# Attention with a relative bias, then a maxout FFN: the left-over keys' band by DMA, one pair loaded straight, one pair's bands and the first FFN block moved

## The chip, the cores and the metric

One core of one Trainium2 chip. The metric is the device time of one execution in microseconds; the kernel before has three timed runs.

## The reference

Eight batches of eight heads, 576 positions, 64 columns per head. Scores get a bias that depends on the distance of query and key alone (32 buckets, all distances from 128 on in one), then softmax, then the values. The result, 4608 tokens of 512, goes through a maxout FFN.

```python
scores = scale * np.matmul(q, k.transpose(0, 1, 3, 2))
...
bias = bias_table[bucket]
scores = scores + bias.transpose(2, 0, 1)[None, :, :, :]
attn = np.exp(scores - np.max(scores, axis=-1, keepdims=True))
attn = attn / (np.sum(attn, axis=-1, keepdims=True) + 1e-09)
x = np.matmul(attn, v)   # then (tokens, heads * columns)
h = np.maximum(np.maximum(x @ w1, x @ w2), x @ w3)
out = h @ w_out
```

## The kernel before, in words

**Attention.** Heads go in pairs, `hp` 0 to 3; the text calls them pair 0 to pair 3. Queries and keys lie transposed in `qT` and `kT`. For each pair PE (TensorE) makes scores with the keys on the partitions (`sc`), ACT (ScalarE) takes their exponential into `e4` (`e` in the profile), and DVE (VectorE) multiplies in the bias as exp(bias) (`times_band`, `times_band_pair`). Only a band around the diagonal needs that, since far distances share one bucket, whose bias has been taken off. The band's factors are in `hank`, one window of 384 columns for each partition and head, loaded by SP (SyncE) from a small DRAM tensor `w_dr` with a step of one element from partition to partition, and read backwards. Then PE sums the values (`attend`, tile `a`; a column of ones gives the divisor), and DVE divides (`quotients`, a reciprocal and a product into `x_sb`).

**The left-over 64 positions.** 576 is 4 x 128 + 64. The left-over keys of both heads of a pair share one tile: `left_keys` makes their scores (`sct`), ACT writes `el`, and `times_bandt` (L905) multiplies its last 192 columns with `bandt`, whose upper 64 partitions hold the even head and lower 64 the odd one. `make_bandt` (L352) fills `bandt` by two copies on POOL (GpSimd) from `hank`, backwards, so that `times_bandt` reads it forwards. `left_queries` and `times_band_left` do the left-over queries (`scq`).

**FFN.** Blocks of tokens go through three gates (`w_bf`, tiles `ps`): the first product of a block (f) is copied by ACT, the second (m) and third (g) are combined with it by DVE. `add_ffn` puts the products of a block of tokens into `pending`, and `fill(n)` emits them on PE up to a budget of n, between attention's steps. For the first 256 tokens the list is f0; f1 and m0; m1; f2 and m2, and the g's come with the next tokens. f's tile, and that of the transposes `xp` and `tp` of the first batch, come from the same two PSUM banks `ff`.

**Order.** The order on PE, DVE, and for most DMAs is that of the program text. Batch 0 has two passes over its pairs: the first makes the scores of the first 256 queries, the second (the loop behind `products`, L1128) the scores of the other queries, pair by pair, and in between the sums for the first 256. `more_transposes(hp + 1)` there turns the next pair's queries on PE into an `ff` bank, and DVE copies them out (L126, `qT<-tp`). `x_transposes` turns divided results into `xT` for the FFN, with a copy by ACT (L123, `xT<-xp`). In the second pass `bands(2)` stands behind the first quotients of pair 0's step, `bands(3)` behind its second ones, and `add_ffn(0, QS)` with `fill(8)` in pair 3's step.

**Batch 1.** (Batch two in the change's title.) Its queries and keys are not turned by DMA as those of later batches but by PE: `second_transposes(made, hp)` puts a pair into an `sc` bank, DVE copies out the queries and ACT the keys (`kT<-tp`). `load_second` (L1072) loads them on POOL's queue with wider rows (`load_packed`: per partition and head 256 neighbouring elements) into a borrowed part of `xT`, first pair 0, then the rest, and `spread_packed` copies each pair to its place: pair 0 on POOL, the others on DVE. Between them it loads the left-over rows, the second gate's weights and, behind all, values and the third gate's weights.

**Queues.** POOL issues the loads of attention and weights, SP the large band, later the DMA transposes and stores. Each load has one of eight semaphores of its queue kind in turn, and waits for the load that had it before. `go_behind` makes a load wait for an instruction.

Of the kernel before, what the change touches and what calls it, by code (L numbers as in the profile page):

```python
# [12 lines left out]
ALU = mybir.AluOpType  # L13
# [26 lines left out]
def kernel(  # L40
# [12 lines left out]
    nc = tc.nc  # L53
    B, H, S, D = q.shape
    d_model, d_ff = moe_w1.shape
    NB = bias_table.shape[0]
    P = 128
    assert d_model == H * D and S == 576 and D == 64 and NB == 32 and H == 8
    inv_sqrt_d = 1.0 / float(np.sqrt(D))
    HP = H // 2  # L60
    QS = 2 * P
    QM = 2 * QS
    KT = 4
# [8 lines left out]
    BAND = 3 * P  # L72
    HALF = 2 * P - 1
    WL = 2 * HALF + 1
# [17 lines left out]
    inorder = tc.keep_in_program_order  # L92
# [82 lines left out]
    def load_q_tail(b):  # L175
        dst = qtail[b % 2][0 : S - KT * P].rearrange("p g (h d) -> p (g h) d", h=2)
        return in_turn(b, nc.gpsimd.dma_start(out=dst, in_=q[b, :, KT * P : S, :].rearrange("h p d -> p h d")), 64 * H)
# [7 lines left out]
    def load_tail(src, b, h0, h1, dst):  # L185
        return [
            in_turn(
                b, nc.gpsimd.dma_start(out=dst(b, par, h0, h1), in_=tail_part(src, b, h0, h1, par)), 32 * (h1 - h0)
            )
            for par in range(2)  # L190
        ]
# [21 lines left out]
    def go_behind(loads, behind):  # L213

        for load in loads if behind else ():
            tc.add_manual_dep(
                load.ins, behind.ins.name,
                mybir.DependencyInfo(mybir.DependencyClass.Sync, mybir.DependencyReason.DATA),
                reason="these loads go behind the transposes in line",
            )  # L220
# [15 lines left out]
    def load_32(src, h, dst, eng, nt=KT):  # L236
# [4 lines left out]
    k_1, q_1 = (  # L241
        xT[:, c, NTOK - KT * H * D :].rearrange("p (h t d) -> p h t d", t=KT, h=H) for c in (3, 2)
    )

    def load_packed(src, h0, h1, dst):
        part = src[1, h0:h1, 0 : KT * P, :].rearrange("h (p t) d -> p h (t d)", t=KT)
        inorder(nc.gpsimd.dma_start(out=dst[:, h0:h1].rearrange("p h t d -> p h (t d)"), in_=part))

    def spread_packed(hp, eng):
        h = slice(2 * hp, 2 * hp + 2)  # L250
        for dst, src in zip(batch[1], (q_1, k_1)):
            inorder(eng.tensor_copy(dst[:, :, h, :], src[:, h].rearrange("p h t d -> p t h d")))
# [5 lines left out]
    batch = [None] * B  # L258
# [77 lines left out]
    w_dr = dram.tile([H, WL], BF16, name="w_dr")  # L336
# [12 lines left out]

    bandt = const.tile([P, HP, 192], BF16, name="bandt")  # L350

    def make_bandt():  # L352
        for par in range(2):
            r = slice(64 * par, 64 * par + 64)
            c = BAND // 2 - 64 * par
            inorder(nc.gpsimd.tensor_copy(bandt[r, :, :], hank[r, par::2, c : c + 192][:, :, ::-1]))

# [334 lines left out]
    def add_ffn(t0, nt, last=False):  # L694
        portions, left = ffn(t0, nt, last)
        portions[0] = rest + portions[0]
        rest[:] = left
        pending.extend((sum(n for n, _ in p), [fn for _, fn in p]) for p in portions)
# [206 lines left out]

    def times_bandt(hp, el):
        return inorder(nc.vector.tensor_tensor(
            out=el[:, S - 192 : S], in0=el[:, S - 192 : S], in1=bandt[:, hp, :], op=ALU.mult
        ))

    def left_queries(hp, qT, kT, el):
# [12 lines left out]
    divided = {}  # L924
# [100 lines left out]
    def x_transposes(hp, half):  # L1025

        xp = ps_f.tile([P, 2 * CH], BF16, tag="ff", name="xp")
        lo, hi = (0, QS) if half == 0 else (QS, S)
        for q in range(lo // P, -(-hi // P))[::-1]:
            c = min(P * q, S - P) - lo  # L1030
            tr(xp[:, c : c + P], x_sb[0][:, q, P * hp : P * hp + P], ident[:])
        act_copy(xT[:, hp, lo:hi], xp[:, 0 : hi - lo])
# [8 lines left out]
    def next_late():  # L1041
        return late.pop(0)() if late else (lambda: None)
# [20 lines left out]
    def load_w(i):  # L1063
        src = (moe_w1, moe_w2, moe_w3)[i].rearrange("(c p) f -> p c f", p=P)
        for f0, f1 in ((0, QS), (QS, d_ff)) if i else ((0, d_ff),):
            in_turn(0, nc.gpsimd.dma_start(out=w_bf[i][:, :, f0:f1], in_=src[:, :, f0:f1]))
# [3 lines left out]
    wo_bf = const.tile([P, FCH, d_model], BF16, name="wo_bf")  # L1070

    def load_second():  # L1072
        for h0, h1 in ((0, 2), (2, H)):
            load_packed(k, h0, h1, k_1)
            load_packed(q, h0, h1, q_1)
            if h0 == 0:
                load_q_tail(1)
                load_tail(k, 1, 0, H, k_diag)
                load_w(1)
                make_bandt()  # L1080
        spread_packed(0, nc.gpsimd)
        load_v(1, 0, H)
        load_w(2)

# [3 lines left out]
    def bands(hp):  # L1088
        times_band_pair(hp, first_e[hp], 0, 0)
        times_band(hp, first_e[hp], 2, 0, QS, inorder)  # L1090
# [9 lines left out]
    for hp in range(HP):  # L1100
        qT, kT = (x[:, hp, :] for x in qk[0])
        e4, el = e_tiles()
# [29 lines left out]
    for hp in range(HP):  # L1132
        qT, kT = (x[:, hp, :] for x in qk[0])
        if begun:
            e4, el = begun.pop()
            more_transposes(hp + 1)
            scores(qT, kT, e4, 1, 2)
        else:
            e4, el = e_tiles()
            visit(qT, kT, e4, [(1, 0), (1, 2)], (lambda: more_transposes(hp + 1)) if hp + 1 < HP else None)  # L1140

        def keys():
            left_keys(hp, qT, kT, el, QS, S)

        def queries():
            left_queries(hp, qT, kT, el)

        def late_bands(hp=hp, e4=e4):
            times_band(hp, e4, 1, QS, QM, inorder)
            times_band_pair(hp, e4, 2, QS)  # L1150

        if hp == 0:
            keys()
        if hp == 1:
            x_transposes(0, 0)
        quotients = next_late()
        if hp < 2:
            quotients()
            if hp == 0:
                bands(2)  # L1160
            else:
                behind.pop()()
                keys()
            queries()
            if hp == 1:
                x_transposes(1, 0)
            else:
                begun.append(e_tiles())
                scores(*(x[:, 1, :] for x in qk[0]), begun[0][0], 1, 0)
            quotients = next_late()  # L1170
            quotients()
            if hp == 0:
                bands(3)
            behind.append(lambda late_bands=late_bands, hp=hp, el=el: (late_bands(), products(hp, el)))
        else:
            if behind:
                behind.pop()()
            if hp == 3:
                quotients()
                add_ffn(0, QS)  # L1180
                fill(8)
            keys()
            if hp == 2:
                quotients()
            queries()
            late_bands()
            if hp == 2:
                x_transposes(2, 0)
                x_transposes(3, 0)
            else:  # L1190
                begin_qk(2)
                x_transposes(0, 1)
                fill(8, lambda: second_transposes(qk[1], 0))
            products(hp, el)
        late.append(lambda hp=hp, e4=e4, el=el: attend(0, hp, e4, el, 1))
# [235 lines left out]
```

## Time and profile before

| | us |
|---|---|
| median of three runs | 308.22 |
| lowest, highest | 306.51, 308.97 |
| the profiled execution | 307.46 |
| its span, first to last instruction | 305.7 |
| PE busy | 294.5 |
| DVE busy | 206.9 |
| ACT busy | 201.3 |
| POOL busy | 143.7 |

In the profile PE is TensorE's matmuls, DVE VectorE, ACT ScalarE, POOL GpSimd, SP SyncE; L and a number is a line of the kernel. A row of a timeline gives the start in microseconds from the span's start, the time that it took (for a count over one from the first start to the last end), engine, line, operation, out<-in by the program's names, the shape and the count. Neighbouring rows of one engine overlap a little, since the next instruction begins while the last one's writes end. In the list of DMA issues the last column is the time from issue to landing in microseconds.

### The profile page before, as it was taken

How to read it: one execution, taken by the hardware profiler on the slowest of the kernel's cores; microseconds unless marked ns; L12 is line 12 of the kernel's file. 1: busy time of each engine (PE TensorE's matmuls, PEld its weight loads, DVE VectorE, ACT ScalarE, POOL GpSimd, SP SyncE). 2: the span in 40 equal slices, each digit the busy share in tenths (PEclk: the TensorE clock that was granted, in tenths of full speed). 3: DMA queues.
4: the chain of work that ended last, by engine and by line, in shares of the span. 5: the costliest groups of instructions: out<-in, count | busy, mean ns of one | idle time of the engine just before them, and what ended most of it. 6: DMA issues, size and time to landing. Idle time of an engine off the chain costs nothing.

```text
span 305.7 us, 10992 instructions
## 1 busy us (share of the span) xinstructions
PE 294.5 (96%) x4736; PEld 183.6 (60%) x4745; DVE 206.9 (68%) x455; ACT 201.3 (66%) x270; POOL 143.7 (47%) x199
## 2 busy tenths in 40 slices
PE   8778999999999999999999999999999999999995
PEld 2356878775556576667666766676667654444442
DVE  6489688787767767776777677767776765453552
ACT  3997998987786677768776877677777720222211
POOL 8998786725739655865686669460000000000000
PEclk9999999999999999999999999999999999999999
DMA  9999999999999999999999999999543013202003
GB/s 158 195 197 194 177 144 144 98 163 122 217 152 129 147 197 168 161 133 200 152 159 127 192 180 146 128 197 153 49 84 135 11 36 91 90 0 105 35 0 137
DMA packets 165777, 40.51 MB, mean 133 GB/s; under 512 B 154585, under 2 KB 161249, under 8 KB 165729
## 3 DMA queue, kind: packets, MB, share of 16 engines
q0 software_dynamic: 105664, 16.66, 96.6%
q1 hardware_dynamic: 58304, 22.69, 40.8%
q8 instruction: 37, 0.61, 0.9%
q10 hardware_dynamic: 1760, 0.47, 0.7%
q14 instruction: 12, 0.09, 0.2%
HBM read 35.39 MB, written 9.45 MB: 147 GB/s over the span
## 4 chain that ended last, share of the span: by engine, by line
PE 87%; ACT 6%; DVE 4%; issue 1%; DMA 1%; DVEq 0%; ACTq 0%
PE psp L109 36%; PE ps L109 17%; PE a L109 14%; PE sc L109 9%; PE pso L109 6%; ACT e L827 4%; PE sct L109 2%; PE warm L109 1%; PE scq L109 1%; DVE e L807 1%; ACT el L827 1%; DVE qT L126 1%; DMA out_dram<-osb 1%; DVE e L822 1%; PE tp L113 1%
## 5 line engine op out<-in xcount | busy, mean ns | idle before, releaser
L827 ACT ACTIVATE e<-sc 128x1024 bf16<-128x1024 f32 x128 | 129.0, 1026 | 29.6 <-PE sc L109 28.3
L109 PEld LDWEIGHTS <-w_bf 64*128 64x128 bf16 (+1 forms) x1112 | 75.9, 95 | 55.1 <-issue 1.5
L109 PE MATMUL psp<-xT,w_bf 64*128 64x512 bf16 x784 | 97.2, 376 | 0.0
L807 DVE TENSOR_TENSOR e<-e,hank 128x512 bf16<-128x512 bf16 (+2 forms) x120 | 57.7, 486 | 13.9 <-ACT e L827 13.2
L109 PE MATMUL ps<-xT,w_bf 128*128 128x512 bf16 (+1 forms) x324 | 58.9, 332 | 0.3
L109 PE MATMUL sc<-qT,kT 64*128 64x256 bf16 (+1 forms) x352 | 48.6, 319 | 2.4 <-ACT e L827 1.1
L199 POOL DMA_DIRECT2D k_sb<-in_k_dram x48 | 36.2, 768 | 18.3 <-DMA vx<-in_v_dram 10.6
L109 PE MATMUL a<-vx,e 64*128 64x65 bf16 (+1 forms) x1664 | 44.7, 190 | 0.0
L109 PEld LDWEIGHTS <-kT 64*128 64x128 bf16 (+1 forms) x712 | 30.1, 94 | 24.2 <-issue 7.1
L109 PEld LDWEIGHTS <-e 64*128 64x128 bf16 (+1 forms) x1664 | 40.7, 95 | 4.2
L199 POOL DMA_DIRECT2D q_sb<-in_q_dram x48 | 36.5, 771 | 11.9 <-DMA k_sb<-in_k_dram 3.0
L109 PEld LDWEIGHTS <-hT 64*128 64x128 bf16 (+1 forms) x462 | 28.2, 95 | 18.7 <-DVE hT L551 1.6
L167 POOL DMA_DIRECT2D vx<-in_v_dram x28 | 24.9, 899 | 23.0 <-DMA vx<-in_v_dram 9.3
L109 PE MATMUL psp<-wo_bf,hT 64*128 64x256 bf16 (+1 forms) x360 | 31.7, 305 | 0.0
L421 ACT ACTIVATE m<-ps 128x512 bf16<-128x512 f32 x14 | 8.4, 597 | 34.3 <-PE ps L109 34.3
L109 PEld LDWEIGHTS <-el 64*128 64x128 bf16 (+1 forms) x676 | 26.4, 94 | 7.0 <-issue 4.4
L827 ACT ACTIVATE el<-sct 128x576 bf16<-128x576 f32 (+2 forms) x36 | 21.7, 605 | 13.1 <-PE sct L109 13.0
L109 PE MATMUL a<-vt,el 64*128 64x65 bf16 (+1 forms) x260 | 29.6, 198 | 0.2 <-DVE m L511 0.2
L551 DVE TENSOR_TENSOR hT<-psp,m 128x1024 bf16<-128x1024 f32 (+1 forms) x20 | 18.7, 956 | 8.2 <-PE psp L109 8.2
L109 PE MATMUL pso<-wo_bf,hT 128*128 128x512 bf16 (+2 forms) x98 | 21.2, 366 | 0.2
L430 DVE TENSOR_TENSOR m<-ps,m 128x512 bf16<-128x512 f32 x14 | 9.7, 692 | 17.0 <-PE ps L109 17.0
L537 DVE TENSOR_TENSOR m<-psp,m 128x1024 bf16<-128x1024 f32 x15 | 18.4, 1224 | 3.3 <-PE psp L109 3.1
(82 smaller groups left out, 291.7 us busy)
## 6 DMA issues: line engine op xcount, KB each, us to landing
out_dram<-osb SPq DMA_DIRECT2D x35, 256.0 KB, 4.1
vx<-in_v_dram POOLq DMA_DIRECT2D x28, 128.0 KB, 6.3
q_sb<-in_q_dram POOLq DMA_DIRECT2D x50, 64.0 KB, 5.0
k_sb<-in_k_dram POOLq DMA_DIRECT2D x48, 64.0 KB, 4.8
w_bf<-in_moe_w_dram POOLq DMA_DIRECT2D x2, 512.0 KB, 8.5
xT<-in_k_dram SPq DMA_DIRECT2D x6, 128.0 KB, 4.6
hank<-w_dr SPq DMA_DIRECT2D x2, 384.0 KB, 4.8
w_bf<-in_moe_w_dram POOLq DMA_DIRECT2D x1, 768.0 KB, 8.4
```

Of the source, the lines that this page charges most:

```text
L109: made = inorder(nc.tensor.matmul(*args, **kw))
L113: inorder(nc.tensor.transpose(*args))
L126: return inorder(nc.vector.tensor_copy(out_, in_))
L167: in_turn(b, nc.gpsimd.dma_start(out=dst[:, t, h0:h1, :], in_=x[:, t, h0:h1, :]), P * (h1 - h0))
L199: in_turn(b, nc.gpsimd.dma_start(out=dst[:, g, :, par, :], in_=part), KT * P)
L421: nc.scalar.activation(out=st[fb]["m0"][:], in_=ps0, func=ACTF.Copy)
L430: inorder(nc.vector.tensor_tensor(out=m[:], in0=ps1, in1=st[fb]["m0"][:], op=ALU.max))
L537: return lambda: inorder(nc.vector.tensor_tensor(out=m[0][:], in0=ps1(), in1=m[0][:], op=ALU.max,))
L551: inorder(nc.vector.tensor_tensor(out=out_[:, i : i + n], in0=ps2()[:, i : i + n], in1=m[0][:, i : i + n], op=ALU.max,))
L807: put(nc.vector.tensor_tensor(out=e4[:, t, :, lo:hi], in0=e4[:, t, :, lo:hi], in1=hank[:, 2 * hp : 2 * hp + 2, c0:c1][:, :, ::-1], op=ALU. ...
L822: inorder(nc.vector.tensor_tensor(out=e4[:, t : t + 2, :, lo : lo + n], in0=e4[:, t : t + 2, :, lo : lo + n], in1=band, op=ALU.mult,))
L827: made = nc.scalar.activation(out=out_, in_=in_, func=ACTF.Exp, scale=inv_sqrt_d)
```

## The change

- `make_bandt` goes. `load_bandt` loads the left-over keys' band by two DMAs on SP's queue from `w_dr`, forwards, behind the product of the first quotients (`divided[0, 0, 0]`); `times_bandt` reads it backwards.
- `load_second` loads pair 0 of batch 1 straight to its place, head by head, by four loads instead of two; POOL's two copies of that pair go. The remaining packed loads move behind the second gate's weights.
- `bands(2)` stands ahead of the first quotients.
- `add_ffn(0, QS)` moves from pair 3's step to the end of pair 2's, with `fill(4)`, ahead of pair 3's scores; `fill(8)` stays where it was.

```diff
-    def make_bandt():
+    def load_bandt(behind):
         for par in range(2):
-            r = slice(64 * par, 64 * par + 64)
-            c = BAND // 2 - 64 * par
-            inorder(nc.gpsimd.tensor_copy(bandt[r, :, :], hank[r, par::2, c : c + 192][:, :, ::-1]))
+            load = inorder(nc.sync.dma_start(
+                out=bandt[64 * par : 64 * par + 64, :, :],
+                in_=bass.AP(
+                    tensor=w_dr.tensor, offset=w_dr.offset + par * WL + BAND // 2,
+                    ap=[[1, 64], [2 * WL, HP], [1, 192]],
+                ),
+            ))
+            go_behind([load], behind)
...
-            out=el[:, S - 192 : S], in0=el[:, S - 192 : S], in1=bandt[:, hp, :], op=ALU.mult
+            out=el[:, S - 192 : S], in0=el[:, S - 192 : S], in1=bandt[:, hp, :][:, ::-1], op=ALU.mult
...
     def load_second():
-        for h0, h1 in ((0, 2), (2, H)):
-            load_packed(k, h0, h1, k_1)
-            load_packed(q, h0, h1, q_1)
-            if h0 == 0:
-                load_q_tail(1)
-                load_tail(k, 1, 0, H, k_diag)
-                load_w(1)
-                make_bandt()
-        spread_packed(0, nc.gpsimd)
+        for src, dst in ((k, batch[1][1]), (q, batch[1][0])):
+            for h in range(2):
+                x = src[1, h, 0 : KT * P, :].rearrange("(p t) d -> p t d", t=KT)
+                inorder(nc.gpsimd.dma_start(out=dst[:, :, h, :], in_=x))
+        load_q_tail(1)
+        load_tail(k, 1, 0, H, k_diag)
+        load_w(1)
+        load_packed(k, 2, H, k_1)
+        load_packed(q, 2, H, q_1)
         load_v(1, 0, H)
         load_w(2)
...
         quotients = next_late()
+        if hp == 0:
+            bands(2)
         if hp < 2:
             quotients()
             if hp == 0:
-                bands(2)
+                load_bandt(divided[0, 0, 0])
...
             if hp == 3:
                 quotients()
-                add_ffn(0, QS)
                 fill(8)
...
             if hp == 2:
                 x_transposes(2, 0)
                 x_transposes(3, 0)
+                add_ffn(0, QS)
+                fill(4)
```

**Where rows move.** DVE, batch 0's second pass, pair 0's step. `e_289` is pair 2's tile, `e_318` pair 3's; `rd` and `x_sb` are the quotients, `qT` the copy of pair 2's turned queries. Before:

```order
L126 COPY qT<-tp_376 128x320
L962 RECIPROCAL rd<-a 128x4
L963 TENSOR_TENSOR x_sb<-a,rd 128x2x128
L822 TENSOR_TENSOR e_289<-e_289,hank 128x4x256
L807 TENSOR_TENSOR e_289<-e_289,hank 128x2x128
L962 RECIPROCAL rd<-a 128x4
L963 TENSOR_TENSOR x_sb<-a,rd 128x2x128
L822 TENSOR_TENSOR e_318<-e_318,hank 128x4x256
L807 TENSOR_TENSOR e_318<-e_318,hank 128x2x128
L126 COPY qT<-tp_456 128x320
```

The same place on DVE now:

```order
L126 COPY qT<-tp_374 128x320
L827 TENSOR_TENSOR e_289<-e_289,hank 128x4x256
L812 TENSOR_TENSOR e_289<-e_289,hank 128x2x128
L967 RECIPROCAL rd<-a 128x4
L968 TENSOR_TENSOR x_sb<-a,rd 128x2x128
L967 RECIPROCAL rd<-a 128x4
L968 TENSOR_TENSOR x_sb<-a,rd 128x2x128
L827 TENSOR_TENSOR e_318<-e_318,hank 128x4x256
L812 TENSOR_TENSOR e_318<-e_318,hank 128x2x128
L126 COPY qT<-tp_456 128x320
```

Pair 2's bands stand ahead of both quotients instead of between them; the rest keeps its order.

ACT, from the end of pair 2's step to batch 1's pair 1. `hT<-ps` are the copies of f0, f1 and f2, which show where those products stand on PE; `kT<-tp` are the copies of batch 1's turned keys, the last tile of exponentials is batch 1's pair 1. Before:

```order
L123 ACTIVATE xT<-xp 128x256 x2
L827 ACTIVATE e_615<-sc 128x2x2x256 x2
L418 ACTIVATE hT<-ps_661 128x512
...
L418 ACTIVATE hT<-ps_704 128x512
...
L123 ACTIVATE kT<-tp 128x512
L123 ACTIVATE kT<-tp 128x128
L418 ACTIVATE hT<-ps_886 128x512
L827 ACTIVATE e_909<-sc 128x2x2x256 x2
```

The same stretch on ACT now:

```order
L123 ACTIVATE xT<-xp 128x256 x2
L423 ACTIVATE hT<-ps_614 128x512
L832 ACTIVATE e_626<-sc 128x2x2x256 x2
L423 ACTIVATE hT<-ps_671 128x512
...
L423 ACTIVATE hT<-ps_803 128x512
...
L123 ACTIVATE kT<-tp 128x512
L123 ACTIVATE kT<-tp 128x128
L832 ACTIVATE e_909<-sc 128x2x2x256 x2
```

f0 stands ahead of pair 3's exponentials, each later block one place sooner, and between the copies of pair 1's turned keys and its exponentials no FFN copy is left.

POOL, from the first gate's weights on. Before:

```order
L1066 DMA w_bf<-in_moe_w_dram 128x4x768
L247 DMA xT<-in_k_dram 128x2x256
L247 DMA xT<-in_q_dram 128x2x256
L177 DMA qtail_98<-in_q_dram 64x8x64
L188 DMA ktail_100<-in_k_dram 64x4x64 x2
L1066 DMA w_bf<-in_moe_w_dram 128x4x256
L1066 DMA w_bf<-in_moe_w_dram 128x4x512
L356 COPY bandt<-hank 64x768 x2
L247 DMA xT<-in_k_dram 128x6x256
```

The same place on POOL now:

```order
L1071 DMA w_bf<-in_moe_w_dram 128x4x768
L1081 DMA k_sb<-in_k_dram 128x4x64 x2
L1081 DMA q_sb<-in_q_dram 128x4x64 x2
L177 DMA qtail_98<-in_q_dram 64x8x64
L188 DMA ktail_100<-in_k_dram 64x4x64 x2
L1071 DMA w_bf<-in_moe_w_dram 128x4x256
L1071 DMA w_bf<-in_moe_w_dram 128x4x512
L247 DMA xT<-in_k_dram 128x6x256
```

Four loads stand where two stood, and the copies are gone.

## Prediction

> **What bounds the kernel now.** I read the page first: which engine is busy, and where it is not.
>
> ```profile
> span 305.7 us, 10992 instructions
> PE 294.5 (96%) x4736; PEld 183.6 (60%) x4745; DVE 206.9 (68%) x455; ACT 201.3 (66%) x270; POOL 143.7 (47%) x199
> PE   8778999999999999999999999999999999999995
> ```
>
> TensorE (PE) is busy for 96% of the span, with holes in the first four slices and the last. All that the change touches runs before 45 us, so I cut that part into stages. The columns are the stage, its length, and the busy time of each engine.
>
> ```profile
> 20.00:30.00 10.00, 7.98 (x158) 6.07 (x154) 9.83 (x28) 8.20 (x14) 9.02 (x12) 1.00 1.41 196
> 30.00:40.00 10.00, 10.00 (x157) 8.22 (x156) 7.66 (x22) 9.54 (x20) 7.74 (x12) 1.00 1.79 182
> ```
>
> From 20 to 30 us PE loses 2.0 us and VectorE (DVE) is full; from 30 us PE is full, and ScalarE (ACT) nearly so. PE's timeline places the hole; in brackets stands the idle time before a row, and what ended it.
>
> ```profile
> 19.79 0.40 PE L109 MATMUL a<-vx,e 128*128 128x65 bf16 x8
> ...
> 21.80 0.29 PE L109 MATMUL scq<-qT,kT 64*128 64x64 bf16 x8 [0.16 <-ACT e L827]
> 23.62 0.27 PE L113 MATMUL xp<-ident,x_sb 128*128 128x128 bf16 x2 [1.53 <-DVE qT L126]
> ...
> 25.66 0.22 PE L109 MATMUL a<-vt,el 128*128 128x130 bf16 x1
> ...
> 26.85 0.29 PE L109 MATMUL scq<-qT,kT 64*128 64x64 bf16 x8 [0.29 <-ACT e L827]
> 27.07 0.40 PE L113 MATMUL xp<-ident,x_sb 128*128 128x128 bf16 x4
> 27.40 0.82 PE L109 MATMUL sc<-qT,kT 64*128 64x256 bf16 x8
> 28.15 0.23 PE L109 MATMUL a<-vt,el 128*128 128x130 bf16 x1
> ...
> 29.06 1.04 PE L109 MATMUL ps<-xT,w_bf 128*128 128x256 bf16 x8
> 29.93 0.30 PE L109 MATMUL sct<-qT,kT 128*128 128x320 bf16 x1
> ...
> 33.18 0.61 PE L109 MATMUL sc<-qT,kT 64*128 64x256 bf16 x8
> ```
>
> The transposes at 23.62 wait for a DVE copy that frees a PSUM bank. On DVE that copy stands behind band products that took longer than their shape needs, and beside them POOL makes the left-over keys' band.
>
> ```profile
> 17.10 0.32 DVE L126 COPY qT<-tp 128x320 bf16<-128x320 bf16 x1
> 18.78 0.18 DVE L962 RECIPROCAL rd<-a 128x4 f32<-128x4 f32 x1 [1.37 <-PE a L109]
> 19.00 0.42 DVE L963 TENSOR_TENSOR x_sb<-a,rd 128x256 bf16<-128x256 f32 x1
> ...
> 20.09 0.91 DVE L807 TENSOR_TENSOR e<-e,hank 128x256 bf16<-128x256 bf16 x1
> ...
> 21.47 1.03 DVE L822 TENSOR_TENSOR e<-e,hank 128x1024 bf16<-128x1024 bf16 x1
> 22.43 0.91 DVE L807 TENSOR_TENSOR e<-e,hank 128x256 bf16<-128x256 bf16 x1
> 23.26 0.31 DVE L126 COPY qT<-tp 128x320 bf16<-128x320 bf16 x1
> ...
> 24.04 0.28 DVE L807 TENSOR_TENSOR e<-e,hank 128x256 bf16<-128x256 bf16 x1
> 24.23 0.68 DVE L822 TENSOR_TENSOR e<-e,hank 128x1024 bf16<-128x1024 bf16 x1
> 24.84 0.25 DVE L907 TENSOR_TENSOR el<-el,bandt 128x192 bf16<-128x192 bf16 x1
> ```
>
> The same two shapes take 0.28 and 0.68 us at 24.04, and 0.91 and 1.03 us three rows earlier: 0.63 + 0.35 + 0.63 = 1.6 us too much.
>
> **Third pair's bands sooner, and no POOL copy.** The bands of pair 2 (the row of 20.09 and the one ahead of it) move ahead of the first quotients, into the 1.37 us in which DVE waited for PE's sums. At the undisturbed 0.80 us (24.04 to 24.84) they run from 17.34 to 18.2, done before 18.78. The next quotients then need not wait for them: the first ones took 0.64 us (18.78 to 19.42), so with PE's sums done at 20.19 (19.79 + 0.40) they end at 20.84, pair 3's bands 0.80 later at 21.6, the copy at 21.9. PE comes to its transposes at 21.80 + 0.29 = 22.09. The whole stall goes: **-1.53 us**. The cover is thin: 0.2 us.
>
> **FFN's first block sooner.** This is the part that I think gives the gain back. PE now does these eight products straight behind the four transposes of 27.07, ahead of the scores of 27.40. They write into the PSUM bank that the third pair's transposes filled, and their fourth product reads the last pair's copy, so they wait for ACT:
>
> ```profile
> 23.93 0.38 ACT L123 ACTIVATE xT<-xp 128x256 bf16<-128x256 bf16 x1 [1.09 <-PE xp L113]
> ...
> 27.67 0.65 ACT L123 ACTIVATE xT<-xp 128x256 bf16<-128x256 bf16 x2
> ...
> 39.12 0.81 ACT L123 ACTIVATE kT<-tp 128x512 bf16<-128x512 bf16 x2
> ```
>
> The first of the two copies ends at 27.67 + 0.38 = 28.05, where PE could have gone on at 27.40: **+0.65 us** (shifts leave the distance as it is, since PE and ACT both start this stretch from the exponentials that end ahead of 26.85). The fourth product comes at 28.05 + 3 x 0.11 = 28.38, the second copy ended at 28.32: no further wait. In return the scores, which took 0.82 for eight at 27.40 against 0.61 at 33.18 because the second four waited for a score bank, come later: **-0.21 us**. The block's own 0.87 us (29.06 to 29.93) is moved, neither won nor lost.
>
> With one block gone ahead, every following block stands one place earlier, and one place is left empty: between the transposes of batch 1's second pair and its scores nothing is left to fill. There the trace of before shows:
>
> ```profile
> 38.48 1.91 PE L109 MATMUL ps<-xT,w_bf 128*128 128x256 bf16 x16
> 40.32 0.61 PE L109 MATMUL sc<-qT,kT 64*128 64x256 bf16 x8
> L123 ACT ACTIVATE kT<-tp 128x512 bf16<-128x512 bf16 x4 | 2.5, 624 | 0.0
> ```
>
> The scores at 40.32 need ACT's copy of the keys, which begins at 39.12 and takes 0.62, so they can begin at 39.75. Sixteen FFN products cover that from 38.48. Without them PE stands from 38.48 to 39.75: **+1.27 us**. ACT cannot be much ahead there, since its exponentials follow the scores that PE makes in the same step; bounds 1.0 (ACT ahead by a quarter of a microsecond) and 1.45 (both copies needed, 39.93).
>
> **The band by DMA.** Two SP loads of 96 KB each (64 partitions x 4 x 192 x 2 bytes), after the first quotients at 19.42, so the second is issued at about 19.9. Where DVE wants it: quotients of pair 2 behind the copy at 21.9 (0.64), late bands (0.80), hence 23.3. DVE is in order; behind the product stand pair 3's quotients and its query copy, and PE's sums (25.66, now 24.13) need the product. No such load is in the trace. Nearest are the loads of the large band, from the same DRAM tensor by the same queue, and an early SP load:
>
> ```profile
> hank<-w_dr SPq DMA_DIRECT2D x1, 384.0 KB, 4.0
> hank<-w_dr SPq DMA_DIRECT2D x1, 384.0 KB, 5.6
> xT<-in_q_dram SPq DMA_DIRECT2D x1, 64.0 KB, 2.4
> w_bf<-in_moe_w_dram POOLq DMA_DIRECT2D x1, 256.0 KB, 7.8
> ktail<-in_k_dram POOLq DMA_DIRECT2D x1, 32.0 KB, 7.0
> ```
>
> That gives 22.3 to 25.5. I take the 4.0 row, whose load is larger but whose neighbours are as busy: landed at 23.9, product done at 24.15, **+0.05 us** on PE; ends 0 and 25.75 - 24.13 = +1.6. Reading the band backwards costs nothing that shows: L920 reads its band backwards already, at 0.22 us for 128 elements, and 0.25 for 192 forwards lies on the same line.
>
> **Batch two's first pair straight.** POOL loses its copies and gets two more issues. Every POOL load waits, by the built order, for the one eight loads before it; the third row is such a wait:
>
> ```profile
> 19.59 1.53 POOL L1066 DMA_DIRECT2D w_bf<-in_moe_w_dram x2
> 21.07 2.13 POOL L356 COPY bandt<-hank 64x768 bf16<-64x768 bf16 x2
> 23.99 0.83 POOL L247 DMA_DIRECT2D xT<-in_k_dram  x1 [0.79 <-DMA xT<-in_k_dram]
> ```
>
> With two loads more ahead of it, the second gate's weights (19.59) become the load that waits until 23.99. Before, their first part landed at 19.59 + 7.8 = 27.4, 1.4 us behind the tails (18.98 + 7.0 = 26.0): the queue, not the issue, set that. Issued at 24.0 they still stand behind the tails, so about 27.8. Wanted: FFN's first block at 28.05 - 1.53 = 26.5, ends 27.4, scores 0.61, sums 0.91, second block 0.87: 29.8. **0**; bounds 0 and, at 7.8 after 24.0, +2.1. The first pair itself is wanted behind that gate, at 30.7 or later, and the rest keeps its distance of eight loads.
>
> **Sum:** -1.53 + 0.65 - 0.21 + 1.27 + 0.05 = +0.23, say **+0.2 us**. The profiled execution took 307.46 (its span of 305.7 and 1.8 around it), so 307.7 there; the median of the three runs is 308.22, which lies 0.8 above, so I forecast **308.4 us**: no change that a measurement of this kernel can tell, which is about 1%, 3.1 us (its three runs lie between 306.51 and 308.97).
>
> **Rivals.** *A, the gain is kept:* ACT runs ahead by enough that neither new wait appears. For it: ACT sat idle 1.09 us ahead of 23.93, so it has time in hand when PE comes earlier. Against: ACT's copies follow PE's own transposes in both places. Then -1.53 - 0.21 = -1.7: 306.5. *B, the band lands late:* its price begins at a landing of 23.85 (product 24.1) and goes one to one onto PE, since DVE's queue and PE's sums both stop. At the 5.6 row +1.6, at 7.0 after 19.9 (what the small loads of the full software queue took) +3.0: from 310 to 311.4, slower. For it: the queue beside it is full of weights at 20 us; against: the loads of SP took 2.4 to 5.6 everywhere. *C, weights late:* second block's gate waits, up to +2.1, 310.5. *D, the slow DVE rows are not POOL's doing:* the row at 20.09 began 1 us before POOL's copy is shown to begin. Then pair 3's bands still end late (1.0 us more), the copy at 22.9, and 0.8 us of the stall stays: 309.2.
>
> The Trainium skill (DMA: Bandwidth & Descriptors, section "Queues, rings and completion order") says that each DMA engine takes its queues in turns, packet by packet. By that rule the band's loads get turns between the weights' long packets, which is case B, and what it costs stands there; the trace agrees so far as the large band's two loads landed after 4.0 and 5.6 us between software loads. The skill's page SBUF — State Buffer, section "Who interferes with whom", says that a two-input DVE operation and a GpSimd copy exclude one another for a whole instruction; by it case D falls away, and the trace agrees but for the start of the row at 20.09.
>
> **Chances.** Forecast 0.58, A 0.17, B 0.13, C 0.05, D 0.07. A, D and the forecast lie within 1%; B passes 1% only with the band 8 us under way, or together with C: slower 0.07. Faster by more than 1% would need 3.1 us where all of PE's holes from 20 to 30 us make 2.0: 0.04. That leaves 0.89. The range reaches to A below and to B's 5.6 row above, each with a little of the spread of runs: 306.2 to 310.4.
>
> **What would show it.** PE's wait at the second pair's head transposes, before 23.62, is gone; a new one of 0.5 to 0.9 us on ACT's xT copy stands ahead of the first FFN block, and one of 1.0 to 1.45 us on kT ahead of batch 1's second pair's scores near 40 us, which begin at 40.3 to 40.7 as before. DVE's 128x256 band products all take 0.28. The band's product waits under 1 us. I am wrong if those scores begin before 39.3 (no new waits) or after 41.5 (band or weights late), or if anything behind 45 us changes.

## The result: slower by 1.45%

The changed kernel takes 312.31 us (median of 4 runs, 310.47 to 313.41) against 308.34 us for the kernel before in runs on the same chip (306.51 to 308.97): ratio 1.0145, 95% interval 1.0107 to 1.0183. Its profiled execution took 312.64 us, 5.2 us more than the 307.46 of before. First its page: the span, the busy times and the clock row.

```profile
span 310.9 us, 10993 instructions
PE 297.5 (96%) x4736; PEld 185.3 (60%) x4745; DVE 204.7 (66%) x455; ACT 201.5 (65%) x270; POOL 141.9 (46%) x197
PEclk9997899999999999999999999999999999999999
```

PE's share is the same 96%, but it is busy 3.0 us longer (297.5 against 294.5) with the same 4736 matmuls: some ran slower. The clock row says where: two digits below 9, between 23 and 39 us. PE's timeline of the changed kernel at the places that the prediction speaks of:

```profile
22.02 0.28 PE L113 MATMUL xp<-ident,x_sb 128*128 128x128 bf16 x2
...
23.82 0.41 PE L109 MATMUL a<-vx,e 128*128 128x65 bf16 x8
26.71 0.29 PE L109 MATMUL a<-vt,el 128*128 128x130 bf16 x1 [2.49 <-DVE el L912]
26.80 0.64 PE L109 MATMUL a<-vx,e 128*128 128x65 bf16 x8
...
29.55 1.86 PE L109 MATMUL ps<-xT,w_bf 128*128 128x256 bf16 x8 [0.43 <-ACT xT L123]
...
45.45 0.61 PE L109 MATMUL sc<-qT,kT 64*128 64x256 bf16 x8 [1.10 <-ACT kT L123]
```

The stall ahead of the transposes is gone (22.02, before 23.62). Then PE stands 2.49 us for DVE's el product. Behind that the same shapes take longer: eight 65-column sums 0.64 us (0.41 at 23.82), eight FFN products 1.86 (1.04 in before). The two waits on ACT follow. Batch 1's second pair's scores begin at 45.45 where before began at 40.32: 5.13 us, which is the whole difference of the spans (310.9 - 305.7 = 5.2). Nothing more is lost behind 45 us. DVE tells what the product waited for, and the view of the DMA issues from 19 to 21 us how long that load was under way:

```profile
22.56 0.69 DVE L827 TENSOR_TENSOR e<-e,hank 128x1024 bf16<-128x1024 bf16 x1
26.40 0.26 DVE L912 TENSOR_TENSOR el<-el,bandt 128x192 bf16<-128x192 bf16 x1 [3.15 <-DMA bandt<-w_dr]
```

```profile
bandt<-w_dr SPq DMA_DIRECT2D x2, 96.0 KB, 6.3
```

The windows show the clock (the column ahead of the last two; the first after the length is PE's busy time):

```profile
24.00:27.00 3.00, 0.51 (x13) 0.40 (x10) 0.57 (x4) 1.20 (x2) 2.53 (x4) 0.95 1.53 175
27.00:33.50 6.50, 6.07 (x67) 4.18 (x64) 3.45 (x12) 3.53 (x7) 5.34 (x8) 0.50 1.37 200
33.50:40.00 6.50, 6.47 (x100) 5.30 (x98) 4.49 (x13) 4.68 (x9) 4.51 (x7) 1.00 1.99 173
```

PE was busy for 0.51 us of 3, and then had half its clock for 6.5 us and 0.3 more at the end of the first window (0.05 x 3 / 0.5): 6.8 us.

The profile also shows how the 6.3 us went. From the issue at 19.44 until 23.5 us the DMA engines moved some 2100 packets of POOL's queue and none of SP's; the band's first packets come at 23.6, its last at 26.0. So 4.2 us passed before the band moved at all, while only other packets did, and its own move took 2.4.

### The profile page after: what moved, and what is told of

Read it like the earlier page. It is cut to its first block, busy times and chain, and to the rows that moved or that the text cites. A ratio compares the mean times of both kernels' runs of the same rounds, so it can differ in the third digit from the quotient of the medians.

```text
span 310.9 us, 10993 instructions
## 1 busy us (share of the span) xinstructions
PE 297.5 (96%) x4736; PEld 185.3 (60%) x4745; DVE 204.7 (66%) x455; ACT 201.5 (65%) x270; POOL 141.9 (46%) x197
## 4 chain that ended last, share of the span: by engine, by line
PE 86%; ACT 7%; DMA 3%; DVE 2%; issue 1%; SPq 0%; DVEq 0%; ACTq 0%
PE psp L109 36%; PE ps L109 17%; PE a L109 13%; PE sc L109 8%; PE pso L109 6%; ACT e L832 5%; PE sct L109 2%; DMA bandt<-w_dr 2%; ACT el L832 2%; PE warm L109 1%; PE scq L109 1%; DMA out_dram<-osb 1%; PE tp L113 1%; ACT xT L123 0%; DVE kT L126 0%
## 5 line engine op out<-in xcount | busy, mean ns | idle before, releaser
L812 DVE TENSOR_TENSOR e<-e,hank 128x512 bf16<-128x512 bf16 (+2 forms) x120 | 56.2, 473 | 14.0 <-ACT e L832 13.4
L109 PE MATMUL ps<-xT,w_bf 128*128 128x512 bf16 (+1 forms) x324 | 59.7, 335 | 0.7 <-ACT xT L123 0.4
L109 PE MATMUL a<-vx,e 64*128 64x65 bf16 (+1 forms) x1664 | 45.6, 191 | 0.0
L109 PEld LDWEIGHTS <-e 64*128 64x128 bf16 (+1 forms) x1664 | 41.5, 95 | 4.2
L167 POOL DMA_DIRECT2D vx<-in_v_dram x28 | 24.8, 893 | 23.6 <-PE a L109 8.7
L542 DVE TENSOR_TENSOR m<-psp,m 128x1024 bf16<-128x1024 f32 x15 | 18.4, 1225 | 3.3 <-PE psp L109 3.2
```

What stands on the lines that cost most here:

```text
L109: made = inorder(nc.tensor.matmul(*args, **kw))
L167: in_turn(b, nc.gpsimd.dma_start(out=dst[:, t, h0:h1, :], in_=x[:, t, h0:h1, :]), P * (h1 - h0))
L542: return lambda: inorder(nc.vector.tensor_tensor(out=m[0][:], in0=ps1(), in1=m[0][:], op=ALU.max,))
L812: put(nc.vector.tensor_tensor(out=e4[:, t, :, lo:hi], in0=e4[:, t, :, lo:hi], in1=hank[:, 2 * hp : 2 * hp + 2, c0:c1][:, :, ::-1], op=ALU. ...
```

## The experiments

**Theory:** the band's load is issued too late and lands at 26.3 us; PE stands for it, its clock then halves; FFN's two waits come on top as predicted. **Rivals:** FFN's move or the straight loads are the loss; or the half clock costs nothing by itself. The runs come from three chips; each is held against before on its own chip, where it took 307.2 to 307.4 us (medians). In the table, "stall" is PE's wait ahead of the transposes (1.53 us in the profile of before), "band wait" its wait for DVE's product with the band, and xT and kT are its two waits on ACT's copies.

| run | against before, 95% interval | what its profile shows |
|---|---|---|
| changed kernel again | 1.0149 (1.0103 to 1.0194) | band wait 2.37, half clock |
| band early | 1.0053 (1.0028 to 1.0078) | no band wait, full clock |
| band early, FFN back | 1.0066 (1.0034 to 1.0098) | waits for loads |
| changed, PE kept busy | 1.0105 (1.0074 to 1.0136), again 1.0073 (1.0048 to 1.0098) | full clock |
| before + only band by DMA | 1.0106 (1.0072 to 1.0141) | band wait 2.50, half clock |
| before + only bands sooner | 0.9992 (0.9964 to 1.002) | stall 0.49 |
| before + only straight loads | 1.0019 (0.9989 to 1.005) | stall 1.39, loads late, no wait for them |
| before + only FFN sooner | 1.0059 (1.0031 to 1.0087) | xT 0.74, kT 1.10 |
| bands sooner + band early | 0.9975 (0.9941 to 1.0009) | waits for DMA |
| changed, packed loads | 1.0143 (1.0097 to 1.0189) | band wait 2.59, half clock for 3.4 us |
| bands sooner, POOL copy sooner | 1.0001 (0.9973 to 1.003) | stall 0.49, waits for DMA |
| with one load less: before; bands sooner + band early; band early, FFN back; changed | 0.9989; 0.9944; 0.9993; 1.0152 | below |

**Band early.** The load goes right behind the large band's.

```diff
     for h0 in (0, KT):
         load_hank(h0, h0 + KT)
+    load_bandt(None)
...
-            if hp == 0:
-                load_bandt(divided[0, 0, 0])
-            else:
+            if hp:
                 behind.pop()()
```

> The changed kernel, but the left-over keys' band is loaded right behind the large band (no wait for the first quotients), so it is in SBUF long before DVE wants it. Theory (the late band and the half clock behind it are the loss): PE's wait on DVE's el product (2.49 us in the changed kernel) falls under 0.3, the granted clock stays full between 20 and 40 us, the two waits on ACT (xT near 28 us, 0.4; kT near 40 us, 1.1) stay; time = before - 1.6 + 0.4 + 1.1 - 0.2, about 308.1 us, within 0.3% of before. Rival (FFN's move or the straight loads of batch two are the loss): still about 312, at least 1% above before. Rival (the loads beside a full software queue hold the end up wherever they are issued): a wait of over 1 us on the band or on the large band stays.

Measured 309.29 us, 1.0053. PE's timeline of this run at the same places, and one more wait:

```profile
22.08 0.28 PE L113 MATMUL xp<-ident,x_sb 128*128 128x128 bf16 x2
...
26.57 1.03 PE L109 MATMUL ps<-xT,w_bf 128*128 128x256 bf16 x8 [0.63 <-ACT xT L123]
...
40.66 0.61 PE L109 MATMUL sc<-qT,kT 64*128 64x256 bf16 x8 [1.10 <-ACT kT L123]
...
69.53 1.46 PE L109 MATMUL pso<-wo_bf,hT 128*128 128x512 bf16 x6 [0.76 <-DMA wo_bf<-in_moe_w_out_dram]
```

The wait on the band and the half clock are gone, and the scores begin at 40.66: 0.34 behind before, where the prediction had put them (40.3 to 40.7). Up to 45 us the theory holds: 45.45 - 40.66 = 4.8 us came from the late band. But the time is 1.6 us above before, not level with it. One more wait stands at 69.53, for a weight load.

**Band early, FFN's block back in its old place.** As the run above, and:

```diff
             if hp == 3:
                 quotients()
+                add_ffn(0, QS)
                 fill(8)
...
                 x_transposes(3, 0)
-                add_ffn(0, QS)
-                fill(4)
```

> As the run with the early band, and FFN's first block put back to its old place; what is left of the change is the third pair's bands sooner, the straight loads and a DMA band that comes in time. Theory: the waits on ACT (xT, kT) are gone as well, only the -1.6 us of the removed stall are left: about 306.7 us, 0.5% below before. Rival (FFN's move costs nothing by itself): same time as the early band alone, within 0.5 us. Rival (straight loads cost): not below before.

1.0066: a miss; as one rival had it, the time is within 0.5 us of the run above (308.83 and 309.29). The stall and both ACT waits are gone, and yet nothing is gained. Three rows of its timeline say why:

```profile
40.60 0.23 PE L109 MATMUL a<-vt,el 128*128 128x130 bf16 x1 [1.38 <-DMA vt<-in_v_dram]
...
112.44 0.39 PE L109 MATMUL sc<-qT,kT 64*128 64x512 bf16 x2 [0.47 <-DMA kT<-k_sb]
...
121.69 0.39 PE L109 MATMUL sc<-qT,kT 64*128 64x512 bf16 x2 [1.26 <-DMA kT<-k_sb]
```

PE comes early and waits 3.1 us for loads and for the turning of later keys. Before has no such wait. So the theory lacked a part: behind PE stand the DMA transfers as a **second bound**. It predicts that what PE gains early is lost to DMA, the more so the later the loads run.

**PE kept busy in the stall.** The changed kernel with zeros multiplied while it waits, in one attention tile; on two chips, on the second beside the changed kernel itself.

```diff
         x = ps_a.tile([P, 6, AW], F32, tag="a", name="a")
+        if (b, hp, half) == (0, 0, 1):
+            for _ in range(20):
+                mm(x[:, 0:4, :], lhsT=zeros[:, 0:P], rhs=zeros[:, 0 : 4 * AW])
```

> The changed kernel with 20 matmuls on zeros (260 columns, about 0.11 us each, 2.2 us together) ahead of the attention sums that wait for the band; their bank is overwritten by the sums. The stall itself stays: the sums still begin near 26.7 us. Theory (the idle stretch costs a second time, by the clock): granted clock stays full from 27 to 34 us, and the time falls by about 2.8 us against the changed kernel, to about 309.5. Rival (the clock in the records follows from something else, or costs nothing, since PE waits for others anyway): time stays near 312.3, or the clock still drops.

> The changed kernel as it is, again, so that the other runs of this call stand beside it on one chip. About 1.0145 of before (1.011 to 1.018), clock halved for some 7 us from near 26.7 us on.

> The changed kernel with the 20 matmuls on zeros in PE's stall, again, beside the changed kernel on the same chip. Theory (half clock costs about 2.8 us): 2 to 3 us below the changed kernel, clock full. Rival (the clock's loss is mostly hidden by the loads' pace behind it): under 1 us below the changed kernel.

Changed 311.96, with zeros 309.82 beside it: 2.1 us by the medians, 1.0149 - 1.0073 = 0.76% or 2.3 us by the ratios; on the first chip the ratio was 1.0105, which is 1.4 us less than the changed kernel's 1.0149. The band lands no earlier: DVE's product begins at 26.22 with the zeros and at 26.06 without. The same two windows of the second zeros run:

```profile
24.00:27.00 3.00, 2.92 (x43) 2.56 (x40) 0.75 (x4) 1.21 (x2) 1.66 (x3) 1.00 1.19 105
27.00:33.50 6.50, 5.76 (x94) 4.45 (x92) 4.35 (x15) 4.76 (x9) 5.79 (x8) 1.00 1.21 163
```

PE busy, clock full: the idle stretch is what halves the clock, and that costs some 2 us on top of the stall. The changed kernel's own ten executions point the same way: the two with a mean granted clock of 0.993 took 310.5 and 310.7 us, the eight with 0.987 to 0.989 took 311.8 to 314.0. A mean higher by 0.005 is some 3 us less at half clock (0.005 x 310 / 0.5), so its length differs between executions of one kernel. (One exception: of the changed kernel with one load less, below, the one execution at 0.995 was no faster, 312.1 us among 311.6 to 312.8.) The rival that it costs nothing falls; my 2.8 was somewhat too much.

**Each part alone.** Before with one part of the change.

> The kernel before with the band's DMA alone (issued behind the first quotients, read backwards, no POOL copy); bands, FFN block and loads as before. Theory: the POOL copy's disturbance of DVE goes (-1.6 us), but PE waits 2 to 3 us for the band and its clock halves for some 6 us (+2.8): about 311 to 312, 1% above before, with no wait of 1 us on kT near 40 us. Rival (the loss needs FFN's move or the straight loads): 306.7 to 308.5.

The band alone (load behind the first quotients, read backwards, no POOL copy) gives 310.15, 1.0106. Its timeline, two of DVE's rows (pair 3's bands), and its window from 27 us on:

```profile
21.62 0.29 PE L113 MATMUL xp<-ident,x_sb 128*128 128x128 bf16 x2
...
26.33 0.23 PE L109 MATMUL a<-vt,el 128*128 128x130 bf16 x1 [2.50 <-DVE el L912]
```

```profile
20.43 0.68 DVE L827 TENSOR_TENSOR e<-e,hank 128x1024 bf16<-128x1024 bf16 x1
21.03 0.29 DVE L812 TENSOR_TENSOR e<-e,hank 128x256 bf16<-128x256 bf16 x1
```

```profile
27.00:33.50 6.50, 5.91 (x77) 4.38 (x78) 5.67 (x18) 4.42 (x9) 5.58 (x8) 0.74 1.49 193
```

Neither FFN's move nor the straight loads are needed for this loss. A mean clock of 0.74 over 6.5 us is half clock for 3.4 us (6.5 x 0.26 / 0.5), half as long as in the changed kernel's profile; two of this run's six executions have a mean clock of 0.989, as low as there, and four 0.993 or 0.994.

The first row shows more. `bands(2)` has its old place here, and yet the transposes come at 21.62 with no wait, and the bands take 0.68 and 0.29. Without POOL's copy the stall goes by itself; moving the bands wasn't needed for it. The next run is the reverse: bands moved, copy kept.

> The kernel before with the third pair's bands ahead of the first quotients and nothing else; the POOL copy of the band and all loads stay. The fourth pair's bands still run beside POOL's copy, so about half of PE's 1.53 us stall stays: 0.7 us less by PE. Theory (PE's time alone decides): 0.5 to 0.9 us below before, ratio 0.997 to 0.9985. Rival (the loads are a second bound that stands close behind PE all the way to 120 us): the stall shrinks as well, but waits for DMA (V of batch 1 near 40 us, keys near 112 to 122 us) take it back, ratio 1.000.

The edit moves `bands(2)` ahead of `quotients()` for the first pair. 0.9992: no gain that shows. Its profile has the stall at 0.49, as expected, and no wait on DMA, so the rival's reason isn't seen either. The 0.49 stands beside POOL's copy, where one band took 0.91. What shows besides is that the stall of before is not always 1.53: the run with FFN alone, which changes nothing ahead of it, has

```profile
21.86 0.27 PE L113 MATMUL xp<-ident,x_sb 128*128 128x128 bf16 x2 [0.19 <-DVE qT L126]
...
26.61 1.03 PE L109 MATMUL ps<-xT,w_bf 128*128 128x256 bf16 x8 [0.74 <-ACT xT L123]
...
40.71 0.61 PE L109 MATMUL sc<-qT,kT 64*128 64x256 bf16 x8 [1.10 <-ACT kT L123]
```

since POOL's copy, which began at 21.07 in before, begins there behind a load that POOL had to wait for:

```profile
17.77 0.71 POOL L247 DMA_DIRECT2D xT<-in_q_dram  x1 [1.12 <-DMA vx<-in_v_dram]
...
21.86 1.78 POOL L356 COPY bandt<-hank 64x768 bf16<-64x768 bf16 x2
```

> The kernel before with FFN's first block one step sooner and nothing else. By the prediction's steps: a wait on the xT copy near 28 us (0.4 to 0.7), a shorter score wait (-0.2), a wait of 1.0 to 1.45 on kT near 40 us: 1.3 to 1.7 us above before, ratio 1.0045 to 1.0055. Rival (by the two runs with the early band, which lie within 0.15% of each other, FFN's move is free): ratio within 0.002 of 1.

308.97, 1.0059 or 1.8 us, with the two waits that the prediction named (0.74 and 1.10). FFN's move is not free; that it seemed so between the two early-band runs fits the second bound, which takes what either of them gains.

> The kernel before with the straight loads of batch two's first pair alone (POOL's copy of the band put ahead of the second gate's weights, so that it need not wait with them). The second gate's weights are issued at 23 to 24 us instead of 19.6, since POOL waits for the load eight before. Theory (this wait lets the queue run dry and all later loads slip by 1 to 2 us): batch 1's V lands 1 us or more later than the 37.7 of before, and PE waits for keys near 112 to 122 us: 0 to 1.5 us above before. Rival (straight loads cost nothing): V lands within 0.4 us of before, ratio 1.000 within 0.002.

The straight loads alone give 1.0019, unclear. They do make the loads late. POOL's timeline of this run at the second gate's weights and batch 1's V tails, with the row of the DMA view for those tails (last column, issue to landing), and then the same two of before:

```profile
24.27 1.51 POOL L1066 DMA_DIRECT2D w_bf<-in_moe_w_dram  x2 [0.94 <-DMA w_bf<-in_moe_w_dram]
...
30.86 0.71 POOL L188 DMA_DIRECT2D vt<-in_v_dram  x1
32.24 0.62 POOL L188 DMA_DIRECT2D vt<-in_v_dram  x1 [0.67 <-DMA w_bf<-in_moe_w_dram]
```

```profile
vt<-in_v_dram POOLq DMA_DIRECT2D x2, 32.0 KB, 8.9
```

```profile
30.42 1.29 POOL L188 DMA_DIRECT2D vt<-in_v_dram  x2
```

```profile
vt<-in_v_dram POOLq DMA_DIRECT2D x2, 32.0 KB, 6.9
```

Those tails land at about 40.4 (the mean of the two issues, 31.5, and 8.9) instead of 37.6 (issued at 30.42 and some 0.6 behind it, and 6.9). With four loads where two stood, the second gate's weights wait for the load eight before them (24.27 instead of 19.59), and less moves meanwhile. The window from 24 to 26 us, last column GB/s, the one ahead of it the DMA engines' share: before, straight loads alone, and (third) the run with early band and FFN back.

```profile
24.00:26.00 2.00, 2.00 (x46) 1.42 (x43) 1.97 (x9) 1.46 (x3) 1.87 (x3) 1.00 1.54 193
```

```profile
24.00:26.00 2.00, 2.00 (x45) 1.42 (x43) 1.97 (x8) 1.38 (x3) 1.73 (x3) 1.00 1.02 68
```

```profile
24.00:26.00 2.00, 1.68 (x35) 1.15 (x31) 1.97 (x8) 1.95 (x5) 1.29 (x2) 1.00 1.65 110
```

193 GB/s fall to 68 and 110. Two causes are mixed here. With the straight loads alone the share falls as well (1.54 to 1.02): the queue runs dry. In the third row the share is as high as in before (1.65), but 1662 of 1663 packets are under 512 bytes (382 of 952 in before), since a straight load moves rows of 64 elements where a packed one moves 256. How much of the delay comes from the wait and how much from the small packets, no run separates. PE comes to that V at 41.04 us in before, so 40.4 is not late there; with PE 1.6 us ahead it is.

**Bands sooner and band early, with packed loads.** Before with `bands(2)` sooner and the early DMA band.

> The kernel before with the third pair's bands sooner and the band by DMA right behind the large band; packed loads, POOL's copies of them and the FFN block as before. The stall of 1.53 us goes, the second gate's weights are issued near 20 us as before. Theory (with the early band it was the straight loads' issue wait that let the queue run dry and the loads slip by 2.6 us): batch 1's V lands less than 1.2 us later than in before, no wait for it over 0.3 us, and most of 1.5 us is kept: ratio 0.995 to 0.998. Rival (the band's 192 KB alone, or the loads' pace in any case, take the gain back): waits of 1 us or more on DMA, ratio 0.999 or more.

0.9975, interval 0.9941 to 1.0009: better by 0.9% than the early-band run with straight loads and FFN in its old place (1.0066), from which it differs by the straight loads alone. The queue stays full (178 GB/s from 24 to 26 us) and V is in time; its loads differ from the other run's in packet size as well as in number. But in its profile two waits on DMA transposes, which turn results and later keys, take back 1.4 us of the 1.5:

```profile
76.45 1.04 PE L109 MATMUL psp<-xT,w_bf 64*128 64x512 bf16 x8 [0.91 <-DMA xT<-x_sb]
...
120.27 0.39 PE L109 MATMUL sc<-qT,kT 64*128 64x512 bf16 x2 [0.49 <-DMA kT<-k_sb]
```

**Changed kernel with packed loads.** The straight loads undone, all else as changed.

> The changed kernel with the straight loads undone (packed loads and POOL's spreading copies of batch two's first pair as in before); late band, FFN move and bands stay. Theory (straight loads cost only where PE comes to the loads early, and here the stall and the half clock keep it late): as the changed kernel within 0.3%. Rival (straight loads cost 0.9% by themselves, as between the two runs with early band and FFN in its old place): about 1.005 of before.

1.0143 against 1.0149: where PE is held up by the band, no cost of the straight loads shows. The two profiles aren't alike, though: with packed loads the half clock lasts 3.4 us instead of 6.8, and PE waits 0.81 us more for DVE while POOL spreads the packed pair. So the equal times fit the theory that the costs of PE and of the loads don't add, and don't prove it.

**Bands sooner, POOL's copy sooner.** No DMA added.

```diff
                 load_q_tail(1)
+                make_bandt()
                 load_tail(k, 1, 0, H, k_diag)
                 load_w(1)
-                make_bandt()
```

> The kernel before with the third pair's bands ahead of the first quotients and POOL's copy of the band put ahead of the key tails' loads, so that it runs from about 18.4 to 20.5 us, between the third and the fourth pair's bands on DVE; no DMA is added. Theory (the stall was the copy's collision with the band products, and with no byte added the loads stay where they were): stall of 1.53 us gone, V and weights land as in before, 1.0 to 1.5 us below before, ratio 0.995 to 0.997. Rival (the copy now slows the quotients or the loads bind all the same): ratio 0.998 or more, with a wait on DVE near 20 us or on DMA behind 40 us.

1.0001, a miss; the rival's waits came. POOL's copy came at 19.37, not 18.4, since POOL waited 1.13 us for a load; it still met the fourth pair's bands (one took 0.91), the stall was 0.49, and two waits on keys near 111 and 119 us (0.34 and 0.45) took most of the rest.

**One load less.** Four kernels without the load of FFN's third weight matrix, to test the second bound by itself.

```diff
     w_bf = [const.tile([P, DCH, d_ff], BF16, name=f"w{i}_bf") for i in range(3)]
+    w_bf[2] = w_bf[1]
...
         load_v(1, 0, H)
-        load_w(2)
```

> The kernel before without the load of FFN's third weight matrix (768 KB); its products read the second matrix instead, so that PE does the same work and the output differs. All later loads run some 3 to 4 us earlier. Both theories: PE bounds here, within 0.2% of before; a clear gain (0.3% or more) would say that the loads bind before already.

> Third pair's bands sooner and the band by an early DMA, packed loads, FFN's block in its old place, and FFN's third weight matrix not loaded (the second is read instead; the output differs). Theory (the loads' pace took the gain): waits on DMA behind 40 us are gone and the 1.5 us come out, ratio 0.995 against before, 1.3 us or more below the same kernel before without that load. Rival (the gain is lost otherwise): 0.9975 as with the load.

> The run with early band, straight loads and FFN's block back in its old place, now without the load of FFN's third weight matrix (the second is read instead; the output differs). Theory (straight loads cost by their place in the queue alone): from 1.0066 to 0.995 to 0.997, with at most the wait for batch 1's V near 40 us left, whose load stands ahead of the one left out. Rival: 1.004 or more.

> The changed kernel without the load of FFN's third weight matrix (the second is read instead; the output differs). Theory (its loss is the late band, the half clock and FFN's two waits, all ahead of that load): unchanged, 1.012 to 1.016 of before, clock halved for some 7 us. Rival (loads behind 40 us hold it up): below 1.010.

Before: 0.9989 (0.9966 to 1.0013), PE bounds there. Bands sooner and band early: 0.9944 (0.9920 to 0.9967), 305.67 us, its waits on DMA all gone; 1.4 us come out against before without that load (307.07). Early band with straight loads: from 1.0066 to 0.9993 (0.9969 to 1.0017), short of the 0.997 that I had expected, with the one wait left whose load stands ahead of the one left out:

```profile
40.45 0.23 PE L109 MATMUL a<-vt,el 128*128 128x130 bf16 x1 [1.02 <-DMA vt<-in_v_dram]
```

Changed: 1.0152 (1.0116 to 1.0188), as with the load; its loss does not need the loads. So the second bound is shown, by early band with straight loads above all: leaving the load out takes away its waits behind 100 us and 0.73%, and the two intervals lie apart, while before gains 0.11%. With packed loads the same edit is worth 0.25% with the load, and 0.45% where neither kernel loads it; there the waits vanish, but the intervals overlap.

## Why the prediction was wrong, point by point

- **The band by DMA** is the step that failed. It took the 4.0 us of the large band's row from 19.9, landing at 23.9, +0.05. The two loads took 6.4 and 6.1 us from 19.44 and 20.18, landing at 26.3. The price from 23.85 on was right: product at 26.40, sums at 26.71, against the 24.13 that the sum had reckoned: +2.6. The range did name this as case B, with 3.0 us at a time of 7.0, but gave it 0.13, since "the loads of SP took 2.4 to 5.6 everywhere". The large band's first packets came 1.3 us after its issue at 10.96, the left-over band's only after 4.2: size was not the term that mattered, but the time until the first packet, which the sum had as part of the 4.0. The Trainium skill (DMA: Bandwidth & Descriptors, section "Queues, rings and completion order") has the engines take the queues in turns, packet by packet. The 6.3 us lie where case B put them, but the trace agrees with turns only from 23.6 us on, when both queues move; in the 4.2 us before, SP's queue got none. Why, the runs don't show. The same two loads issued 8 us earlier were under way for 6.4 and 7.2 us; there they had the time.
- **A cost that no part of the prediction had:** behind the stall PE ran at half clock for 6.8 us. It cost some 2 us, shown by the zeros (1.4 and 2.3 by the ratios). Case B priced the stall one to one; up to 45 us it cost 4.8, nearly twice its 2.5.
- **Third pair's bands sooner, and no POOL copy:** right in outcome. Transposes at 22.02 (predicted 22.09), stall gone, all 128x256 bands up to 28 us at 0.28 or 0.29. But the sum credited both edits together, and the copy's removal is enough: the band's DMA alone, with the bands in their old place, has no stall, while the bands moved beside the copy leave 0.49. Case D falls with it. And 1.53 was one execution's stall; two kernels with nothing changed ahead of it show 0.19 (FFN alone) and 0.55 (before with one load less), and what is won there is lost to loads.
- **FFN's first block sooner and the missing cover:** right. The waits stand where they were put, 0.43 to 0.74 on xT and 1.10 on kT (1.27 taken, bounds 1.0 to 1.45); alone 1.8 us by the ratio against +1.71 (0.65 - 0.21 + 1.27).
- **Straight loads:** no cost shows in the changed kernel, as taken, where PE was late; the reason given was right for the weights' issue (23.44, 24.0 predicted) but overlooked that less moves behind it, and that the later loads have little slack. That costs 0.9% in a kernel whose PE is early.
- **The sign that would show it wrong** came out: the scores began at 45.45, behind the 41.5 that was named for a late band.

In sum, from the profiles: -1.6 (stall) + 2.65 (band, 26.71 - 25.66 + 1.6) + 0.43 (xT) + 1.10 (kT) makes 2.6 of the 5.1 us; the other 2.5 us, by subtraction, are the half clock less the shorter scores. The medians give 4.0 us (312.31 - 308.34): 2.9 us for the late band with its clock (1.0149 - 1.0053, net of what the kernel with the early band then loses to loads), the rest mostly FFN's move. These shares are read from separate runs and add up only roughly, because of the second bound.

What stays open: no version here that loads all it needs beats before for sure. Bands sooner with an early band lies at 0.9975, its interval reaching over 1. Open too are why the band's first packet came so late, and which part of the straight loads' delay is small packets.

## What to carry to other kernels

Ask of a new DMA not how large it is but what is queued beside it, and how long it may be until its first packet, and issue it as soon as its source exists: the same 192 KB cost 2.9 us at 19 us and left no wait of their own at 12. Price a stall of PE above its length when it comes near 2.5 us, because the clock behind it may halve. Before crediting a gain to one of two edits, run each without the other. And where loads run at full share next to a PE at 96% (the page of before has 9 in the first 28 of the 40 slices of its DMA row), a gain on PE must be held against the landing times of the next loads, which a run with one load left out brings to light.

## What was unexpected of the hardware

- An idle stretch of 2.3 to 2.6 us was enough to halve the granted clock in all five profiles that have it, for 6.8 us in three and 3.4 us in two (the band's load alone, and packed loads). The Trainium skill (TensorE: Matmul & The Clock Gate, section "Why this matters for your kernels") advises against idle gaps above some 3 us; here a shorter one did it.
- Loads of 96 KB on SP's queue took 5.4 to 7.2 us from issue to landing beside POOL's queue in all runs, the large band's 384 KB 4.0 to 5.6 in before. In the changed kernel 4.2 us of it passed ahead of the first packet.
- POOL's wait for the load eight before, with the straight loads' small packets ahead of it, brought 193 GB/s down to 68 for 2 us, and batch 1's V came 2.8 us later.
